# Output stores as planned entries, and a new planned order, in a fused attention and token-mixing kernel

## The chip, the cores and the metric

The kernel runs on one core of a Trainium2 chip. The time is the device time of one execution in microseconds; the median of several runs is shown, and the profile is that of one execution. PE is TensorE (PEld its weight loads), DVE is VectorE, ACT is ScalarE, POOL is GpSimd, and SP is the queue that issues nearly all DMAs here.

## The reference

Two parts, one behind the other. Attention with a sigmoid in place of the softmax, over 8 batches, 12 heads, 448 positions and 64 dimensions; then a token-mixing MLP on its output `x` (8 x 448 x 768):

```python
scores = scale * np.matmul(q, k.transpose(0, 1, 3, 2)) - np.log(S)
attn = 1.0 / (1.0 + np.exp(-scores))
x = np.matmul(attn, v)                      # heads side by side: (B, S, 768)
...
W_tok = scale * np.einsum('bsd,btd->bst', x @ w_q, x @ w_k)
mixed = np.einsum('bst,btd->bsd', W_tok, x)
out = np.maximum(mixed, 0.0) @ w_out
```

Inputs and output are float32. The kernel computes the matrix products in bfloat16 and never forms `W_tok`: it multiplies `x @ w_k` into `x` first (a 64 x 768 product, `tmp`), and then `x @ w_q` into that.

## The kernel before

A batch is a *unit* u (8 of them), four heads are a *quad* j (3 per unit), so there are 24 quads n = 0 to 23. For each quad, q, k and v are loaded as float32 (448 KB each), cast to bfloat16, and q and k are transposed so that the head dimension lies on the partitions. Transposing is done in one of several ways that a letter picks: on PE with a copy out of PSUM (L291, L286, L276), or on DVE in 32 x 32 blocks (L259), for which POOL swaps blocks first (L157 to L163), or on DVE by halves (L252, L228).

Each quad has 7 steps of scores (`scores`, L303: four matmuls on 64 x 64 quarters of the array, then one sigmoid of 128 x 896 on ACT, L308) and 7 steps of values (`values`, L321, summed in PSUM, then a copy to `xt`, L330). So there are 168 sigmoids. Behind a quad, `xt` is transposed back to `xn` (`tr_x`, L344 and L361). Behind a unit come the products of the MLP: `mlp_wqk` (L387, L400), `mlp_wkn` (L416), `mlp_tmp` (L431, copy L435), `mlp_mix` (L471, L483; relu on DVE at L459 or on ACT at L457), and the output blocks (`out_chunk` L600, `out_pair` L516, `out_halves` L556), which are copied out of PSUM into a tile `o` (L525, L633) and stored. There are three such tiles, and in the tail the load buffers `ld` serve as output tiles too.

PSUM is handed out as four pairs of banks in a fixed rotation (`free2`). A step that takes a pair waits until the copy or the sigmoid that read it last has finished.

The order of all work is written out by hand as a string, `PLAN`, one letter for each step: S is a step of scores, P and p one of values (copy on DVE or ACT), q, k and other small letters transposes, X and x `tr_x`, W and L `mlp_wqk`, N, U and M the further products, O and I output blocks (small letter: copy on ACT), C a move of output weights, F a matmul on zeros. Each engine runs its instructions in the order in which the letters emit them and waits only for what it needs. A second string, `ORDER`, gives the order of loads and casts, and a dot in it hands that cast to DVE; the others go to POOL. Loads use a ring of six buffers: the load of entry i is emitted on SP when entry i - 6 has been cast, and so stands in SP's queue between the stores of output blocks. Before, an output block's store is emitted on SP at once behind its copy (L534, L571, L614), so a load that is emitted later waits in SP's queue until that copy has been made.

Of the kernel before, what the change touches and what calls it, by code (L numbers as in the profile page):

```python
# [9 lines left out]
F32 = mybir.dt.float32  # L10
# [7 lines left out]
def kernel(  # L18
# [12 lines left out]
    nc = tc.nc  # L31
    B, H, S, HD = q.shape
    D = H * HD
    DH = moe_w_q.shape[1]
    assert DH == HD == 64 and S == 448 and D == 768
    P = 128
# [83 lines left out]
    def xt(u, j):  # L120
# [4 lines left out]


    PLAN = (
        "SSSFFFFKSqSFFSSkFFSPSPPSpPPPSFSqSkSFPppSPpSpPSabSXSpPSpPSprS"
        "XPPSSFSSWWWSsWzWXWSpPPSpNSppPSqSkSUSXSMSppPSPMppSPSSqkpSSppP"
        "pSpSPWWcSWXSMSdWXSWWSpPSPppNSPPqSkSSUxSMSPPSPppSPPSOOSMSooSq"  # L130
        "kSOoMCSPPCPcSppPPSSdoOSSoXSSOLLScLLLSLpppSPppPSSdoOSOSNxSOcS"
        "UdrSCPSPpSPPPCPpPSPpPSpSsOPSXoSMzSooLSxLSLLLLSPpPSPpPcSPSoXS"
        "SdOOoSpMPSPpCpPSPSoNMSYCOxScPPdppSSooppSPSoOSxScUSLLLSLLdLSp"
        "ppSpPpcPSdoSOMSoSOSMSPpPSPrppSPOmosSoSzooxOSoSOoSoNSOxSOSUSp"
        "PSMcppdPpcpLLLSppLSppLLSPPpOOSdNOSOxOSomoScOOSodSSoOpPmpPpSP"
        "PSOOSoSOtOSoSOMomppPPpmPPOSoxSoSOSLLcLdLLSoSLOSoSOocSoSxoSdO"
        "SppPPSPpSPOSOoNSOoSoSoxSOpPSptpSpPPPppMmPpPpyMWWWWWWxyiNiiti"
        "iiImiImMIiiOoooOoOoOoOOooOO"
    )
    PLAN = "".join(PLAN)  # L140
    KIND = ["a"] + [t for t in PLAN if t in "qacer"]
# [354 lines left out]
    ot = {}  # L496

    opened = []

    def slot(half, b):  # L500

        return b // 2 + (0 if b % 2 == half else NC)

    def out_pair(act):

        if opened:
            w, blocks, part, fb, ps = opened.pop()
        else:
            w, blocks = chunks.pop(0)
            part = 0  # L510
            fb, ps, _ = bank2()
        mx = mxs[w].rearrange("p (u b x) -> p u b x", u=2, b=12)
        for b in range(3 * part, 3 * part + 3):
            for y, (u, i) in enumerate(blocks):
                for x in range(2):
                    nc.tensor.matmul(  # L516
                        ps[HALF[x], y, 0:NB], mx[HALF[y], u, b, 64 * (i - 3 * y) : 64 * (i - 3 * y) + 64],
                        wout16[HALF[y], slot(y, b), x * NB : (x + 1) * NB],
                        start=(b == 0), stop=(b == 11),
                    )  # L520
        if part < 3:
            opened.append((w, blocks, part + 1, fb, ps))
            return
        o = p_o.tile([P, 2, NB], F32, tag="o", name="o")
        COPY["s" if act else "v"](out=o, in_=ps[:, :, 0:NB])  # L525
        release(fb)
        (u0, i0), (u1, i1) = blocks
        for x in range(2):
            cols = slice(x * NB, (x + 1) * NB)
            if u0 == u1:  # L530
                dst = out[2 * w + u0].rearrange("(p i) d -> p i d", i=NI)[:, i0 : i1 + 1 : i1 - i0, cols]
            else:
                dst = out[2 * w : 2 * w + 2].rearrange("b (p i) d -> i p b d", i=NI)[i0, :, :, cols]
            nc.sync.dma_start(out=dst, in_=o[HALF[x]])  # L534

    def out_halves(act):

        if opened:
            w, m, part, fb, ps = opened.pop()
        else:  # L540
            w, m, nb = chunks.pop(0)
            assert nb < 0
            part = 0
            ot[0] = (
                ld_next()[:, 0:D].rearrange("p (b x) -> p b x", b=2) if len(cast) == len(ORDER) + 2
                else p_o.tile([P, 2, NB], F32, tag="o", name="o")
            )
        o = ot[0]
        b, h = divmod(part, 2)
        if not h:  # L550
            fb, ps, _ = bank2()
        for c in range(3 * h, 3 * h + 3):
            t0 = 2 * S * c + m * P + b * NP
            for y in range(2):
                for x in range(2):
                    nc.tensor.matmul(  # L556
                        ps[HALF[x], y, 0:NB], mxs[w][HALF[y], t0 : t0 + NP], wout16[HALF[y], c, x * NB : (x + 1) * NB],
                        start=(c == 0), stop=(c == NC - 1),
                    )
        if h:  # L560
            COPY["s" if act else "v"](out=o[:, b], in_=ps[:, 0, 0:NB])
            nc.vector.tensor_tensor(out=o[:, b], in0=ps[:, 1, 0:NB], in1=o[:, b], op=ALU.add)
            release(fb)
        if part < 3:
            opened.append((w, m, part + 1, fb, ps))
            return
        (b0, i0), (b1, i1) = divmod(2 * m, NI), divmod(2 * m + 1, NI)
        for x in range(2):
            cols = slice(x * NB, (x + 1) * NB)
            if b0 == b1:  # L570
                nc.sync.dma_start(  # L571
                    out=out[2 * w + b0].rearrange("(p i) d -> p i d", i=NI)[:, i0 : i1 + 1, cols], in_=o[HALF[x]],
                )
                continue
            for y, (b, i) in enumerate(((b0, i0), (b1, i1))):
                nc.sync.dma_start(
                    out=out[2 * w + b].rearrange("(p i) d -> p i d", i=NI)[:, i, cols], in_=o[HALF[x], y],
                )

    def out_chunk(act, tail):  # L580

# [10 lines left out]
        last = isinstance(fb, int)  # L592
        if nb == 0 and not part:
            late = w == NU // 2 - 1 and len(cast) == len(ORDER) + 2
            ot[0] = ld_next()[:, 0:D] if late else p_o.tile([P, D], F32, tag="o", name="o")
        o = ot[0]

        def block(ps, w0, w1, c0, c1):
# [35 lines left out]
        release(fb)  # L634
        split = tail and w == NU // 2 - 1 and m == NI - 1
        if nb or split:
            store(slice(nb * NB, (nb + 1) * NB) if split else slice(0, D))

    w32 = {}

# [41 lines left out]
    for n in range(7):  # L682
# [1 line left out]


    ORDER = (
# [5 lines left out]
    )  # L692
    BY = {"s": [], "v": []}
    for x in ORDER.split():
# [5 lines left out]
    ORDER = [(x[0], int(x[1:])) for x in ORDER.replace(".", "").lower().split()]  # L700
    LAG = 9
    issued = {}
    done = dict.fromkeys("SPqkKxWNUMOCgz", 0)
    used, loaded, cast = set(), set(), set()

    ring = [("q", 0), ("k", 0)]
# [105 lines left out]
    for t in PLAN:  # L812
# [14 lines left out]
        if t == "S":  # L827
            scores(*divmod(c, NI))
            cast_by_others()
        elif kind == "P":  # L830
            n, i = divmod(c, NI)
            values(n, i, tail, "s" if t == "p" else "v")
            if i == NI - 1:
                used.add(("v", n))
                pump()
        elif kind in "qk":
            if t in "rs":
                quads_r.append(c) if t == "r" else None
                if t == "s":
                    quadrants(c, 0)  # L840
            tr(c, kind, t)
            if t in "df":
                used.add(("q", c))
            if t not in "cers":
                used.add((kind, c))
                pump()
        elif t == "g":
            move()
        elif t == "z":
            n = quads_r.pop(0)  # L850
            quadrants(n, 1)
            used.update({("q", n), ("k", n)})
            pump()
        elif t == "K":
            tr_part("k", k016, K3, "v")
            tr_part("k", k016, K4, "v")
        elif kind == "x":
            tr_x(c, tail, t in "XY", "s" if t in "yY" else "v")
        elif kind == "W":
            mlp_wqk(*divmod(c, NC), tail, t in "wl", t in "Ll")  # L860
        elif kind == "C":
            for y in range(2):
                nc.sync.dma_start(out=wout16[HALF[y], NC + c, :], in_=wout16[HALF[1 - y], c, :])
        elif kind == "N":
            mlp_wkn(c)
        elif kind == "U":
            (mlp_tmp_tiled if t in "Tt" else mlp_tmp)(c, t in "ut")
        elif kind == "M":
            u, x = divmod(c, NC // 2)
            mlp_mix(u, x, t == "m", tail)  # L870
            if x == NC // 2 - 1:
                if u // 2 in TW:
                    chunks.extend((u // 2, ((u % 2, i), (u % 2, 6 - i))) for i in range(3))
                    if u % 2:
                        chunks.append((u // 2, ((0, 3), (1, 3))))
                else:
                    chunks.extend((u // 2, m, -1) for m in (range(3, NI) if u % 2 else range(3)))
        elif kind == "O":
            if (opened or chunks)[0][0] in TW:
                out_pair(t == "o")  # L880
            elif t in "Ii":
                out_halves(t == "i")
            else:
                out_chunk(t == "o", tail)
    assert not chunks and not opened
# [1 line left out]
_INS = ['q', 'k', 'v', 'moe_w_q', 'moe_w_k', 'moe_w_out']  # L887
_OUTS = [((8, 448, 768), 'float32')]
# [25 lines left out]
```

## Time and profile before

| | |
|---|---|
| median of 3 runs | 187.45 us (186.94 to 189.1) |
| the profiled execution | 187.01 us |
| its span, first to last instruction | 185.3 us |
| instructions | 8549 |
| HBM read, written | 35.78 MB, 11.01 MB |
| clock granted to TensorE | 1.00 |

A row of a group reads: line, engine, operation, out<-in, shapes and count, then busy us and mean ns of one, then the idle time before them and what ended most of it. A row of the timeline reads: start, length, engine, line, operation, tiles, shapes, count, and in brackets the idle time of the engine before it and what released it. A row of the chain reads: start, length, what. A busy PE is not PE at its peak, since matmuls are pipelined.

### The profile page before, as it was taken

How to read it: one execution, taken by the hardware profiler on the slowest of the kernel's cores; microseconds unless marked ns; L12 is line 12 of the kernel's file. 1: busy time of each engine (PE TensorE's matmuls, PEld its weight loads, DVE VectorE, ACT ScalarE, POOL GpSimd, SP SyncE). 2: the span in 40 equal slices, each digit the busy share in tenths (PEclk: the TensorE clock that was granted, in tenths of full speed). 3: DMA queues.
4: the chain of work that ended last, by engine and by line, in shares of the span. 5: the costliest groups of instructions: out<-in, count | busy, mean ns of one | idle time of the engine just before them, and what ended most of it. 6: DMA issues, size and time to landing. Idle time of an engine off the chain costs nothing.

```text
span 185.3 us, 8549 instructions
## 1 busy us (share of the span) xinstructions
PE 174.2 (94%) x3660; PEld 116.8 (63%) x3662; DVE 137.0 (74%) x213; ACT 165.8 (89%) x215; POOL 116.2 (63%) x160
## 2 busy tenths in 40 slices
PE   7887999979989999999999999999999999999990
PEld 7443645544555564656554768768888888879660
DVE  3444787999778899998998999687655885586610
ACT  4798999989989999999999999998999999976540
POOL 1445898699659999799999797969894710000000
PEclk9999999999999999999999999999999999999999
DMA  5999999988998989999999987698388344420696
GB/s 173 360 386 383 285 352 340 388 288 287 375 345 309 283 252 316 367 403 269 300 338 326 264 291 254 203 359 288 115 201 288 80 126 104 117 60 18 165 241 175
DMA packets 26085, 48.51 MB, mean 262 GB/s; under 512 B 3968, under 2 KB 19968, under 8 KB 26048
## 3 DMA queue, kind: packets, MB, share of 16 engines
q1 hardware_dynamic: 25888, 47.79, 79.7%
q8 instruction: 28, 0.46, 1.0%
q10 hardware_dynamic: 160, 0.20, 0.5%
q14 instruction: 9, 0.07, 0.1%
HBM read 35.78 MB, written 11.01 MB: 253 GB/s over the span
## 4 chain that ended last, share of the span: by engine, by line
PE 74%; ACT 12%; DVE 7%; issue 2%; DMA 2%; POOL 0%; ACTq 0%; SPq 0%; DVEq 0%
PE banks L303 15%; PE banks L516 14%; PE banks L321 13%; PE banks L600 12%; ACT at L308 12%; PE banks L387 3%; PE banks L556 3%; PE banks L431 2%; PE banks L344 2%; DMA ld<-in_k_dram 2%; PE banks L361 2%; DVE xt L330 2%; PE banks L400 2%; PE banks L483 1%; PE banks L471 1%
## 5 line engine op out<-in xcount | busy, mean ns | idle before, releaser
L308 ACT ACTIVATE at<-banks 128x896 bf16<-128x896 f32 x168 | 141.1, 929 | 4.5 <-PE banks L303 3.6
L303 PE MATMUL banks<-qk 64*64 64x448 bf16 x672 | 62.6, 357 | 2.8 <-DVE mx L459 0.9
L321 PE MATMUL banks<-at,v 64*64 64x448 bf16 x672 | 45.2, 351 | 0.5 <-ACT at L308 0.2
L303 PEld LDWEIGHTS <-qk 64*64 64x64 bf16 x672 | 25.9, 105 | 20.1 <-issue 11.5
L516 PE MATMUL banks<-wout,mx 64*64 64x384 bf16 x672 | 36.8, 323 | 0.0
L188 POOL CAST qk<-ld 128x896 bf16<-128x896 f32 x25 | 30.5, 1233 | 5.7 <-issue 3.3
L321 PEld LDWEIGHTS <-v 64*64 64x64 bf16 x672 | 23.3, 106 | 9.4 <-issue 2.7
L330 DVE CAST xt<-banks 128x896 bf16<-128x896 f32 x20 | 21.8, 1088 | 7.4 <-PE banks L321 5.6
L516 PEld LDWEIGHTS <-mx 64*64 64x64 bf16 x672 | 24.1, 107 | 3.9
L600 PE MATMUL banks<-wout,mx 128*128 128x384 bf16 (+1 forms) x138 | 24.7, 320 | 0.0
L198 POOL CAST v<-ld 128x896 bf16<-128x896 f32 x22 | 20.6, 949 | 3.6 <-DMA ld<-in_v_dram 2.4
L459 DVE TENSOR_SCALAR mx<-banks 128x1024 bf16<-128x1024 f32 (+2 forms) x19 | 18.6, 987 | 2.3 <-PE banks L471 1.6
L600 PEld LDWEIGHTS <-mx 128*128 128x128 bf16 x138 | 12.0, 97 | 10.7 <-issue 4.5
L157 POOL COPY swap<-qk 32x448 uint32<-32x448 uint32 x26 | 14.7, 564 | 4.9 <-DVE qk L188 3.4
L163 POOL COPY qk<-swap 32x448 uint32<-32x448 uint32 x26 | 15.3, 590 | 1.5
L259 DVE STREAM_TRANSPOSE qk<-qk 128x448 f32<-128x448 f32 x26 | 16.0, 628 | 0.0
L525 DVE COPY o<-banks 128x768 f32<-128x768 f32 x12 | 11.5, 955 | 5.9 <-PE banks L516 3.6
L160 POOL COPY qk<-qk 32x448 uint32<-32x448 uint32 x26 | 14.8, 567 | 1.5
L374 DVE COPY xn<-banks 128x1024 bf16<-128x1024 bf16 (+1 forms) x14 | 8.7, 630 | 2.2 <-PE banks L361 2.0
L457 ACT ACTIVATE mx<-banks 128x448 bf16<-128x448 f32 (+1 forms) x11 | 8.1, 768 | 0.5 <-PE banks L483 0.5
L387 PE MATMUL banks<-xt,wqk 64*64 64x448 bf16 x120 | 8.0, 351 | 0.0
L198 POOL CAST q<-ld 128x896 bf16<-128x896 f32 x6 | 5.6, 932 | 3.8 <-DMA ld<-in_q_dram 2.3
(94 smaller groups left out, 212.6 us busy)
## 6 DMA issues: line engine op xcount, KB each, us to landing
ld<-in_q_dram SPq DMA_DIRECT2D x24, 448.0 KB, 6.0
ld<-in_v_dram SPq DMA_DIRECT2D x24, 448.0 KB, 6.1
ld<-in_k_dram SPq DMA_DIRECT2D x23, 448.0 KB, 6.3
out_dram<-o SPq DMA_DIRECT2D x42, 192.0 KB, 4.7
ld<-in_moe_w_out_dram SPq DMA_DIRECT2D x6, 384.0 KB, 5.7
out_dram<-ld SPq DMA_DIRECT2D x11, 192.0 KB, 2.8
wout<-wout SPq DMA_DIRECT2D x12, 96.0 KB, 5.7
out_dram<-ld SPq DMA_DIRECT2D x4, 96.0 KB, 2.6
```

Of the source, the lines that this page charges most:

```text
L160: eng.tensor_copy(out=w[hi, 0], in_=w[lo, 1])
L163: eng.tensor_copy(out=w[lo, 1], in_=z[lo])
L188: COPY[e](out=f[:, :, "qk".index(nm)].rearrange("p e i d y -> p e y i d"), in_=ld.pop((nm, n)).rearrange("p (y i e d) -> p e y i d", y=2, ...
L198: COPY[e](out=t16.rearrange("p i b d -> p b i d"), in_=ld.pop((nm, n)).rearrange("p b (i d) -> p b i d", i=NI),)
L259: nc.vector.transpose(out=qk[n][:, t].rearrange("p t i n -> p (t i n)").bitcast(F32), in_=w)
L303: nc.tensor.matmul(sc[HALF[h], g, 0:S], qk[n][HALF[g], h, 1, i, :], qk[n][HALF[g], h, 0].rearrange("p i n -> p (i n)"), start=True, stop=True,
L308: nc.scalar.activation(at, sc[:, :, 0:S], ACTF.Sigmoid, bias=attn_bias, scale=attn_scale)
L321: nc.tensor.matmul(ps[HALF[g], h, 0:S], ld["v16", n][HALF[h], i, g, :], ats[n, i][HALF[h], g, :], start=(i == 0), stop=(i == NI - 1),)
L330: COPY[eng](out=xt(u, j)[:, :, 0:S], in_=ps[:, :, 0:S])
L459: nc.vector.tensor_scalar(dst, ps, moe_scale, 0.0, ALU.mult, ALU.max)
L516: nc.tensor.matmul(ps[HALF[x], y, 0:NB], mx[HALF[y], u, b, 64 * (i - 3 * y) : 64 * (i - 3 * y) + 64], wout16[HALF[y], slot(y, b), x * NB : ...
L600: nc.tensor.matmul(ps, mxs[w][:, 2 * S * c + m * P : 2 * S * c + (m + 1) * P], wout16[:, c, w0:w1], start=(c == 0), stop=(c == NC - 1),)
```

## The change

Three things. Stores of output blocks become entries of their own in `PLAN`, with the letter D: `out_pair`, `out_halves` and `out_chunk` no longer issue the store but put it on a list, and D issues the oldest. When a new `o` tile is wanted whose buffer a waiting store still reads, that store is issued first; in the tail stores are issued at once. `PLAN` is another string (647 letters, with 21 D, in place of 627). `ORDER` is another string, with 19 casts on DVE in place of 14. The counts of the other steps stay; some copies change between DVE and ACT, and one quad is transposed by POOL swaps and L259 in place of halves.

```diff
+    stores, o_tiles = [], [0]
+
+    def flush(n=None):
+
+        for _, f in stores[:n]:
+            f()
+        del stores[:n]
+
+    def o_tile(shape):
+
+        while stores and stores[0][0] <= o_tiles[0] - 3:
+            flush(1)
+        o_tiles[0] += 1
+        return p_o.tile(shape, F32, tag="o", name="o")
...
-        o = p_o.tile([P, 2, NB], F32, tag="o", name="o")
+        o = o_tile([P, 2, NB])
         COPY["s" if act else "v"](out=o, in_=ps[:, :, 0:NB])
         release(fb)
...
+        stores.append((o_tiles[0] - 1, store))
+        if tail:
+            flush()
...
+        elif kind == "D":
+            flush(1)
```

The beginning of the two plans and of the two orders of loads, and the order's last lines:

```diff
-        "SSSFFFFKSqSFFSSkFFSPSPPSpPPPSFSqSkSFPppSPpSpPSabSXSpPSpPSprS"
-        "XPPSSFSSWWWSsWzWXWSpPPSpNSppPSqSkSUSXSMSppPSPMppSPSSqkpSSppP"
+        "SSSFFFFFKSSqFFSSkFFSSSSPPpSPppPFqSkSPPPSSppPPSabSXSrSpPppSPS"
+        "DpXSPSSFSSWWsWWzXWWSpPSPPPpNSPqSkSSDUSXSMDSpPPMSPppSPSqkSWSW"
...
-        "q1 .k1 v0 v1 .q2 k2 q3 k3 v2 k4 q4 w0 q5 v3 q6 k5 v4 q7 v5 w5 "
-        ".k6 q8 k7 .w4 .k8 k9 v6 v7 v8 w3 q9 q10 w6 .k10 w1 w2 k11 .v9 "
+        "q1 .k1 v0 q2 k2 v1 k3 q3 v2 q4 k4 w0 v3 v4 q5 k5 v5 q6 q7 k6 w3 "
+        "k7 .k8 .w1 v6 k9 q8 v7 q9 w5 q10 w4 v8 .k10 w2 .w6 .v9 q11 k11 "
...
-        "q21 q22 q23 v20 .v21 v22 v23 k22 .k23 "
+        ".q17 k16 .k17 q18 v16 k18 .k19 q19 k20 v17 v18 .k21 q20 .q21 "
+        ".q22 k22 v19 .v20 q23 v21 .v22 .k23 .v23 "
```

More of the change, by code (lines that the diff above doesn't have):

```diff
@@ L127 @@
     PLAN = (
-        "SSSFFFFKSqSFFSSkFFSPSPPSpPPPSFSqSkSFPppSPpSpPSabSXSpPSpPSprS"
-        "XPPSSFSSWWWSsWzWXWSpPPSpNSppPSqSkSUSXSMSppPSPMppSPSSqkpSSppP"
[L130 to L138, printed above, removed]
+        "SSSFFFFFKSSqFFSSkFFSSSSPPpSPppPFqSkSPPPSSppPPSabSXSrSpPppSPS"
+        "DpXSPSSFSSWWsWWzXWWSpPSPPPpNSPqSkSSDUSXSMDSpPPMSPppSPSqkSWSW"
+        "WcpSpPSppPSPXSWSSdWMXSWSppppSPpNPSqSkSUSxSMPSppPSpSPPSOOSMSO"
+        "oqSkSOOPSMCpSPPppSPDSOcOdDSSOXSLLLSOcSLLpSLppSPpPPSSodOSxSoN"
+        "CSCOCSPPcdSUSPpSDCPrpPpPSpppsSpSCOPSXoSMSOoLzSxLSLDLLSLppSPp"
+        "cPSpPSOodSSOXoMSpPPcSPpPSPSoNMSYOSxSDdoDOPSpPSppSPPOOSxDSUSL"
+        "cLLSSLdLLpPpPSppPcSOSoMSOSOSMPPSPppPDdmOPSoSOSOSOcONSdoxSOOS"
+        "OSxoSOSUSpcpSMPPPPplllSPlDpSdpPlDxlpppDOSoSoSOOSDOcSModSooSO"
+        "OcNSOmTpPpSpPPpSOMoSodSOSOODSPDPSOPPSpPPmOOoDSomcLOSLdLLSLLo"
+        "SoDSoSOSOcodSDOxSOPpSppSPNpPODoSxSoOSoSOxSOSOtPpSPSppPMPPppP"
+        "mPPPMwwwwwwxxIyNiiTiIiImiimmiIIooOOoooooOOoooOO"
     )
@@ L498, with out_pair @@
     opened = []
+    stores, o_tiles = [], [0]
[8 more added lines that the diff above has]
+        return p_o.tile(shape, F32, tag="o", name="o")
     def slot(half, b):
         return b // 2 + (0 if b % 2 == half else NC)
-    def out_pair(act):
+    def out_pair(act, tail):
         if opened:
@@ L527, in out_pair, with store, out_halves @@
         (u0, i0), (u1, i1) = blocks
[L528 to L536, printed above, removed]
+        def store():
+            for x in range(2):
+                cols = slice(x * NB, (x + 1) * NB)
+                if u0 == u1:
+                    dst = out[2 * w + u0].rearrange("(p i) d -> p i d", i=NI)[:, i0 : i1 + 1 : i1 - i0, cols]
+                else:
+                    dst = out[2 * w : 2 * w + 2].rearrange("b (p i) d -> i p b d", i=NI)[i0, :, :, cols]
+                nc.sync.dma_start(out=dst, in_=o[HALF[x]])
+        stores.append((o_tiles[0] - 1, store))
+        if tail:
+            flush()
+    def out_halves(act, tail):
         if opened:
@@ L545, in out_halves @@
                 ld_next()[:, 0:D].rearrange("p (b x) -> p b x", b=2) if len(cast) == len(ORDER) + 2
-                else p_o.tile([P, 2, NB], F32, tag="o", name="o")
+                else o_tile([P, 2, NB])
             )
@@ L567, in out_halves, with store @@
         (b0, i0), (b1, i1) = divmod(2 * m, NI), divmod(2 * m + 1, NI)
[L568 to L578, printed above, removed]
+        def store():
+            for x in range(2):
+                cols = slice(x * NB, (x + 1) * NB)
+                if b0 == b1:
+                    nc.sync.dma_start(
+                        out=out[2 * w + b0].rearrange("(p i) d -> p i d", i=NI)[:, i0 : i1 + 1, cols], in_=o[HALF[x]],
+                    )
+                    continue
+                for y, (b, i) in enumerate(((b0, i0), (b1, i1))):
+                    nc.sync.dma_start(
+                        out=out[2 * w + b].rearrange("(p i) d -> p i d", i=NI)[:, i, cols], in_=o[HALF[x], y],
+                    )
+        stores.append((o_tiles[0] - 1, store))
+        if tail or len(cast) == len(ORDER) + 2:
+            flush()
     def out_chunk(act, tail):
@@ L594, in out_chunk @@
             late = w == NU // 2 - 1 and len(cast) == len(ORDER) + 2
-            ot[0] = ld_next()[:, 0:D] if late else p_o.tile([P, D], F32, tag="o", name="o")
+            ot[0] = ld_next()[:, 0:D] if late else o_tile([P, D])
         o = ot[0]
@@ L636, in out_chunk @@
         if nb or split:
-            store(slice(nb * NB, (nb + 1) * NB) if split else slice(0, D))
+            stores.append((o_tiles[0] - 1, lambda: store(slice(nb * NB, (nb + 1) * NB) if split else slice(0, D))))
+            if tail or w == NU // 2 - 1 and (m == NI // 2 or len(cast) == len(ORDER) + 2):
+                flush()
     w32 = {}
@@ L702 @@
     issued = {}
-    done = dict.fromkeys("SPqkKxWNUMOCgz", 0)
+    done = dict.fromkeys("SPqkKxWNUMOCDgz", 0)
     used, loaded, cast = set(), set(), set()
@@ L879 @@
             if (opened or chunks)[0][0] in TW:
-                out_pair(t == "o")
+                out_pair(t == "o", tail)
             elif t in "Ii":
-                out_halves(t == "i")
+                out_halves(t == "i", tail)
             else:
                 out_chunk(t == "o", tail)
-    assert not chunks and not opened
+    assert not chunks and not opened and not stores
 _INS = ['q', 'k', 'v', 'moe_w_q', 'moe_w_k', 'moe_w_out']
```

3 rows, old and new, of the table ORDER are left out of this document.

## The prediction

> **What bounds the kernel now.** I read the page from the top: busy shares, the chain of waits, a table of four stretches, and the timeline where the chain leaves one engine for another.
>
> ```profile
> span 185.3 us, 8549 instructions
> PE 174.2 (94%) x3660; PEld 116.8 (63%) x3662; DVE 137.0 (74%) x213; ACT 165.8 (89%) x215; POOL 116.2 (63%) x160
> PE 74%; ACT 12%; DVE 7%; issue 2%; DMA 2%; POOL 0%; ACTq 0%; SPq 0%; DVEq 0%
> L308 ACT ACTIVATE at<-banks 128x896 bf16<-128x896 f32 x168 | 141.1, 929 | 4.5 <-PE banks L303 3.6
> 6.20:50.00 43.80, 38.95 (x811) 21.63 (x805) 32.23 (x44) 42.58 (x52) 31.80 (x39) 1.00 0.99 344
> 50.00:110.00 60.00, 59.22 (x1084) 34.29 (x1087) 54.48 (x75) 59.02 (x75) 52.18 (x70) 1.00 0.95 315
> 110.00:161.90 51.90, 51.90 (x1372) 42.50 (x1365) 36.52 (x53) 49.98 (x62) 30.70 (x45) 1.00 0.65 195
> 161.90:185.30 23.40, 19.01 (x364) 14.03 (x358) 11.08 (x23) 11.75 (x25) 0.00 (x0) 1.00 0.52 132
> ...
> 107.61 0.92 ACT at L308
> 112.92 0.97 PE banks L516 x22
> ```
>
> The stretches give length, then busy time of PE, PEld, DVE, ACT and POOL, the clock, and DMA. Until 110 us ScalarE is the metronome: it is busy 42.58 of 43.80 and 59.02 of 60.00 us, mostly with the 168 sigmoids. The last long ScalarE piece of the chain is at 107.61 us; the long pieces behind it are matmuls. From 110 us PE has no gap (51.90 of 51.90 us) while DVE falls to 36.52. So there are two regimes. In front, time is won only where ScalarE stands or steps slowly. Behind, only by fewer matmuls or by coming to that stretch sooner. VectorE is close to a bound in front, with 54.48 of 60.00 us.
>
> The two built programs have the same 7326 PE instructions, the same loads and stores and 168 sigmoids, in another order. No PE work is saved, so the sum goes by ScalarE's lost time in front, and by stands that the new order makes.
>
> **Where ScalarE loses time in front.**
>
> ```profile
> 6.22 11.73 ACT L308 ACTIVATE at<-banks 128x896 bf16<-128x896 f32 x14 [0.48 <-PE banks L303]
> 18.50 20.42 ACT L308 ACTIVATE at<-banks 128x896 bf16<-128x896 f32 x25 [0.55 <-PE banks L303]
> 39.16 0.92 ACT L308 ACTIVATE at<-banks 128x896 bf16<-128x896 f32 x1 [0.23 <-PE banks L303]
> 40.35 11.58 ACT L308 ACTIVATE at<-banks 128x896 bf16<-128x896 f32 x14 [0.28 <-PE banks L303]
> 52.60 5.95 ACT L308 ACTIVATE at<-banks 128x896 bf16<-128x896 f32 x7 [0.67 <-PE banks L303]
> ```
>
> A merged row's last sigmoid starts 0.92 us before the row's end. The 25 from 18.50 us step by (20.42 - 0.92) / 24 = 0.81 us: the undisturbed pace. Three places fall behind it. The first 14 step by (11.73 - 0.92) / 13 = 0.83, and the 15th starts 18.50 - 17.03 = 1.47 us behind the 14th: 0.9 us lost in all. Around 39 us the steps are 39.16 - 38.00 = 1.16 and 1.19: 0.7 us. At 52.60 the step is 52.60 - 51.01 = 1.59: 0.8 us.
>
> **Part 1: loads and casts in a new order.** The first place:
>
> ```profile
> 11.20 0.93 POOL L198 CAST v<-ld 128x896 bf16<-128x896 f32 x1 [0.27 <-DMA ld<-in_v_dram]
> 15.39 0.94 POOL L198 CAST k<-ld 128x896 bf16<-128x896 f32 x1 [3.26 <-DMA ld<-in_k_dram]
> 12.44 0.63 DVE L198 CAST q<-ld 128x896 bf16<-128x896 f32 x1 [1.05 <-DMA ld<-in_q_dram]
> 16.38 0.41 PE L212 MATMUL banks<-ident,k 64*64 64x64 bf16 x28 [0.93 <-POOL k L198]
> 16.92 1.09 DVE L291 COPY qk<-banks 128x1792 bf16<-128x1792 bf16 x1 [1.92 <-ACT at L308]
> ```
>
> POOL waits 3.26 us for k2 to land, PE waits for that cast, and L291 (its copy is what the 15th scores read) follows 0.13 us behind the transposes. These loads are of one size, so landings go by the slot in SP's queue. Before, slots four to six hold v1 (cast at 11.20), q2 (12.44) and k2 (15.39); after, q2, k2 and v1. So k2 can be cast from about 12.4 us, 3 us sooner, and v1 takes the late slot and is done at 16.3. The values of quad 0 move as well, behind the 11th and 12th scores, so k2's transposes are now set by PE's order: an estimated 16.1 us for their end. L291 adds 1.09 and the scores 0.4, so the 15th sigmoid starts near 17.7 instead of 18.50. The change adds a wait: three value steps of quad 1 stand ahead of the 15th scores in PE's queue and wait for v1 until 16.3; at four matmuls in 0.2 us each they are done at 16.9, under the 17.3 of L291. That cover is 0.4 us; without it the gain shrinks by as much as v1 is later. Gain taken: 0.8 us.
>
> The second place:
>
> ```profile
> 35.94 1.21 POOL L188 CAST qk<-ld 128x896 bf16<-128x896 f32 x1
> 36.06 1.57 DVE L198 CAST k<-ld 128x896 bf16<-128x896 f32 x1
> 38.68 0.38 PE L303 MATMUL banks<-qk 64*64 64x448 bf16 x4 [0.94 <-DVE mx L459]
> ```
>
> The cast of k6 on VectorE stands between two L459 copies; the second releases the banks that the scores wait for. After the change k6 is cast by POOL, and nothing stands between the two. What is late next is VectorE's own queue there (xt, then L291 of the next quad).
>
> The third place: at 52.60 the scores wait behind the matmuls of L431, which themselves stand 0.42 us; the chain there reads:
>
> ```profile
> 50.85 0.42 issue
> 51.28 0.66 PE banks L431 x5
> ```
>
> In the new plan a step of scores stands between L431 and the transposes of xt, which before followed it at once. The second and third place hold 0.7 + 0.8 = 1.5 us. I take half, 0.75: the new order also packs two mode changes of PE, a mix and a transpose between the 47th and 48th scores, whose crowding no row of this trace prices; I bound it by 0 and by the 0.8 us of the stands just read.
>
> **Part 2: stores as entries of their own.** A store now stands up to 10 scores behind its copy, and loads may pass it on SP; no more than three output tiles are open, since the oldest store is issued first when a fourth is wanted.
>
> ```profile
> 137.63 0.96 DVE L525 COPY o<-banks 128x768 f32<-128x768 f32 x1 [1.67 <-DMA out_dram<-o]
> out_dram<-o SPq DMA_DIRECT2D x42, 192.0 KB, 4.7
> ```
>
> Before, one copy waited for a store, 1.67 us, inside the stretch in which PE has no gap: it cost nothing. After, the ninth tile (copied after the 122nd scores) is stored after the 132nd and needed again at the 136th. There the scores step by about 1.06 us (51.90 us for 49), and 4 steps are 4.2 us against 4.7 for a landing. So a copy on VectorE may wait 0 to 1.7 us, with L459, xt and the next output copy behind it, whose banks PE wants. In the early half the loads that pass the stores come sooner, by at most a store's place in the queue; POOL's waits there are off the chain (POOL 0%). I take 0 for both: SP goes through its list as its waits end, often earlier than the place in the plan, and the one case seen was free.
>
> Instruction reads:
>
> ```profile
> PEld L303 <- issue: 11.5, 35, 1.2
> q8 instruction: 28, 0.46, 1.0%
> ```
>
> If the 28 reads caused all 11.5 us of PEld's unexplained standing, a plan that avoids them could win up to that in front; but ScalarE stands only 4.5 us in all, three places of which are counted above. Taken: 0. The Trainium skill (Runtime: NRT & Kernel Launch, Instruction fetch mechanics) says that sequential instruction fetch is mostly hidden behind the issue rate, which gives the same 0; no row here ties a stand to a read.
>
> **Part 3: 19 casts on VectorE in place of 14.**
>
> ```profile
> L188 DVE CAST qk<-ld 128x896 bf16<-128x896 f32 x7 | 6.7, 970 | 0.0
> L228 DVE STREAM_TRANSPOSE qk<-qk 32x448 f32<-32x448 f32 x12 | 7.6, 636 | 0.3
> L633 ACT COPY o<-banks 128x384 f32<-128x384 f32 x6 | 3.0, 492 | 0.0
> ```
>
> Through the 120th scores both orders have 12 casts on VectorE. The five more, 5 x 0.97 = 4.9 us, all lie behind, where VectorE has 51.90 - 36.52 = 15.4 us free; one quad fewer by halves takes 4 x 0.64 = 2.5 us off. Hidden, unless they come in one block: two follow the 134th scores and three the 148th. ScalarE copies one output half less in front, 0.4 us off (its 0.49 less the overlap). PE's remaining work at the 120th, 144th and 168th scores differs by a few value steps, so the rear keeps its length.
>
> **The sum.** 0.8 + 0.75 + 0.4 = 1.95 us off. The profiled execution took 187.01 us, 1.7 us of it around the span; the median of the runs is 187.45, 0.44 above. 187.01 - 1.95 + 0.44 = 185.5 us.
>
> **Rivals.** *New stands for old.* ScalarE's lost time is moved, not removed: with VectorE at 54.48 of 60.00 us, 2 us less length means 94% busy, and its in-order queue passes every slip to the banks. Against it: the places above are read from this trace and the new order does treat each. It gives 187.0.
>
> *Blocks of casts stop PE (slower).* At the 134th and 148th scores two and three casts stand in a row, with output and xt copies behind them whose banks PE needs. A cast took 0.97 us on average and 1.57 beside a POOL cast; at the mean of these, 1.27, the blocks are 2.5 and 3.8 us. One step of 1.06 is covered by the other banks, so PE stands 1.5 + 2.7 = 4.2 us, and 185.5 + 4.2 = 189.7. At 0.97 it is 2.7 us and 188.2; from 1.18 us a cast on, it is over 1% slower. Against it: four bank pairs may cover more than one step. The Trainium skill (SBUF — State Buffer, SBUF: two separate sides) has VectorE and GpSimd hold a shared port pair exclusively for a whole instruction, which speaks against more VectorE casts while POOL works. By that rule, the trace agrees: 1.57 us beside POOL.
>
> *More than counted.* All 1.5 us of the second and third place go, and the loads gain something further on: 183.9 us or less.
>
> **How the numbers follow.** Forecast 0.47, about 184.4 to 186.8; new stands 0.26; blocks of casts 0.19; more than counted 0.08. One per cent, about what a measurement of this kernel can tell, is 185.6 and 189.3 us. Faster: 0.27 of the forecast and 0.08 make 0.35. Slower: 0.14 of the blocks. Same: 0.20 + 0.26 + 0.05 = 0.51. The range leaves out half of the best case and the upper part of the blocks: 183.8 to 189.4.
>
> **What would show it.** Right: the 15th sigmoid starts at 17.5 to 17.9 us, POOL's 3.26 us wait is on v, no step over 1.1 us near the 39th and 55th sigmoid, and the 120th starts 1.5 to 2.5 us before 110.8. Wrong: the 120th no earlier; or PE with gaps of a microsecond between 125 and 160 us, on L525 or L330, behind L188 or a store.

## The result, and the profile after

| | before | changed |
|---|---|---|
| median | 186.96 us (20 runs) | 188.38 us (20 runs) |
| profiled execution | 187.01 us, span 185.3 | 189.17 us, span 187.4 |

The changed kernel takes 1.0092 times as long, with a 95% interval of 1.0062 to 1.0121. 185.5 was forecast; it came out 1.4 us slower than before instead of some 2 us faster. All medians here are taken over every run, while ratios leave out disturbed runs, so the two can differ a little.

Lines of the changed kernel are numbered higher (L516 is L530, L525 is L539, L600 is L626, L633 is L659); L303, L308 and L431 keep theirs. The page of the changed kernel, with the rows that answer to those of before:

```profile
span 187.4 us, 8548 instructions
...
PE 175.3 (94%) x3660; PEld 116.4 (62%) x3662; DVE 140.1 (75%) x218; ACT 164.0 (88%) x211; POOL 115.0 (61%) x161
...
q8 instruction: 28, 0.46, 1.0%
...
PE 68%; DMA 16%; ACT 4%; POOL 3%; issue 3%; DVE 3%; SPq 1%; ACTq 0%; POOLq 0%
...
L308 ACT ACTIVATE at<-banks 128x896 bf16<-128x896 f32 x168 | 141.3, 929 | 7.4 <-PE banks L303 6.9
...
L303 PEld LDWEIGHTS <-qk 64*64 64x64 bf16 x672 | 25.6, 105 | 21.3 <-issue 13.2
```

ScalarE's idle time before a sigmoid grew from 4.5 to 7.4 us, nearly all behind the scores on PE. The loads that the chain names (DMA 16%, 2% before) all lie ahead of 40 us, where it is followed back through POOL's casts rather than the sigmoids; they say nothing on the time behind 40 us. To see where, here are four stretches of the changed kernel (length, then busy time of PE, PEld, DVE, ACT and POOL, the clock, DMA share, GB/s):

```profile
45.00:53.00 8.00, 6.92 (x190) 4.10 (x194) 6.31 (x10) 7.23 (x10) 4.41 (x6) 1.00 0.95 349
105.00:110.00 5.00, 4.10 (x92) 2.62 (x87) 3.81 (x5) 3.98 (x6) 4.46 (x8) 1.00 0.88 316
126.00:136.00 10.00, 8.36 (x202) 6.28 (x198) 7.04 (x11) 8.03 (x11) 7.39 (x11) 1.00 0.87 298
...
110.00:162.00 52.00, 50.36 (x1331) 40.82 (x1327) 39.68 (x55) 47.90 (x58) 28.53 (x41) 1.00 0.67 197
```

The first three of the kernel before:

```profile
45.00:53.00 8.00, 7.33 (x183) 4.04 (x182) 5.91 (x9) 7.33 (x10) 4.97 (x7) 1.00 1.00 365
105.00:110.00 5.00, 4.84 (x111) 3.46 (x104) 4.82 (x6) 5.00 (x7) 3.91 (x5) 1.00 0.87 287
126.00:136.00 10.00, 10.00 (x280) 8.56 (x273) 6.93 (x10) 9.45 (x12) 9.09 (x13) 1.00 0.57 180
```

PE now stands inside the stretch that had no gap: 8.36 of 10.00 us, with 202 matmuls where 280 ran, at the same full clock. The DMA engines are 0.87 to 0.95 busy in all three; in the third they were at 0.57 before. In the first two they were as busy before (1.00 and 0.87), so their busy share alone does not make PE stand. The chain of waits of the changed kernel shows what the standing looks like (start, length, what):

```profile
48.83 0.77 PE banks L431 x7
49.60 0.54 issue
50.14 0.32 PE banks L431
...
106.39 0.18 PE banks L303 x3
106.57 0.73 issue
107.30 0.36 PE banks L303
...
127.00 0.18 PE banks L303 x3
127.19 0.80 issue
127.98 0.35 PE banks L303
...
133.21 0.12 PE banks L416 x7
133.33 0.84 issue
134.18 0.19 PE banks L416
```

Each stand lies in the middle of a group: three matmuls of four or seven of eight are done, then PE waits for nothing that the profile shows, and then the last one runs. No copy and no bank can do that, since a group waits for its banks at its first matmul. Counted in pairs of weight load and matmul, the four come in front of pairs 864, 1888, 2400 and 2528; all are 96 past a multiple of 128. So each lies at a multiple of 256 PE instructions from the others (a pair is two), and the span holds 28 instruction reads of 16 KB for 7,322 PE instructions, one for each 262. The trace of DMA ties the reads to these places. The changed kernel's PE passes such a boundary at 100.54 us; the two windows below are 100.5 to 104.8 us and 104.8 to 105.9 us (queue: packets, MB, share of the 16 engines):

```profile
q1 hardware_dynamic: 371, 1.14, 83.8%
...
q1 hardware_dynamic: 133, 0.30, 86.7%
q8 instruction: 1, 0.02, 5.4%
```

For 4.3 us only loads and stores move. Then comes one instruction packet (104.87 to 105.82 us); PE reaches the next boundary at 106.2 and goes on at 107.30, 1.5 us behind the end of the packet. So the block was used up before the next was there. Measured between two weight loads, the four stands are 1.16, 1.08, 1.20 and 0.96 us, 4.4 us in all. (Of the first, 0.31 us is the gap that the same place has where PE doesn't stand, in e2 below.) The kernel before shows one, 0.77 us at pair 864: it is the "0.42 issue" at 50.85 that the prediction quotes.

From 110 to 162 us the changed kernel's PE lacks 52.00 - 50.36 = 1.64 us, and the two stands of that stretch in the chain are 0.80 + 0.84 = 1.64 us: no store, cast or copy made PE stand there. The three stands behind 100 us, which the kernel before doesn't have, are 2.37 us in the chain, and the span is 2.1 us longer.

### The profile page after: what moved, and what is told of

It is laid out like the page before. It is cut to its first block, busy times and chain, and to the rows that moved or that the text cites. A ratio compares the mean times of both kernels' runs of the same rounds, so it can differ in the third digit from the quotient of the medians.

```text
span 187.4 us, 8548 instructions
## 1 busy us (share of the span) xinstructions
PE 175.3 (94%) x3660; PEld 116.4 (62%) x3662; DVE 140.1 (75%) x218; ACT 164.0 (88%) x211; POOL 115.0 (61%) x161
## 4 chain that ended last, share of the span: by engine, by line
PE 68%; DMA 16%; ACT 4%; POOL 3%; issue 3%; DVE 3%; SPq 1%; ACTq 0%; POOLq 0%
PE banks L530 14%; PE banks L303 14%; PE banks L321 12%; PE banks L626 12%; DMA ld<-in_k_dram 7%; DMA ld<-in_q_dram 5%; DMA ld<-in_v_dram 4%; ACT at L308 3%; PE banks L387 3%; PE banks L576 3%; PE banks L431 2%; PE banks L361 2%; PE banks L471 1%; PE banks L344 1%; PE banks L447 1%
## 5 line engine op out<-in xcount | busy, mean ns | idle before, releaser
L308 ACT ACTIVATE at<-banks 128x896 bf16<-128x896 f32 x168 | 141.3, 929 | 7.4 <-PE banks L303 6.9
L303 PE MATMUL banks<-qk 64*64 64x448 bf16 x672 | 63.5, 358 | 3.9 <-issue 1.5
L303 PEld LDWEIGHTS <-qk 64*64 64x64 bf16 x672 | 25.6, 105 | 21.3 <-issue 13.2
L530 PE MATMUL banks<-wout,mx 64*64 64x384 bf16 x672 | 36.4, 323 | 0.0
L188 POOL CAST qk<-ld 128x896 bf16<-128x896 f32 x21 | 25.5, 1222 | 7.3 <-issue 4.2
L530 PEld LDWEIGHTS <-mx 64*64 64x64 bf16 x672 | 23.7, 107 | 6.5 <-issue 2.5
L330 DVE CAST xt<-banks 128x896 bf16<-128x896 f32 x19 | 20.6, 1086 | 7.0 <-PE banks L321 6.5
L626 PE MATMUL banks<-wout,mx 128*128 128x384 bf16 (+1 forms) x138 | 24.9, 321 | 0.2 <-ACT at L308 0.2
L459 DVE TENSOR_SCALAR mx<-banks 128x1024 bf16<-128x1024 f32 (+2 forms) x20 | 19.9, 1000 | 2.3 <-PE banks L471 0.9
L198 POOL CAST v<-ld 128x896 bf16<-128x896 f32 x20 | 18.8, 951 | 2.6 <-DMA ld<-in_v_dram 2.3
L157 POOL COPY swap<-qk 32x448 uint32<-32x448 uint32 x28 | 15.9, 570 | 5.1 <-DVE qk L188 3.6
L626 PEld LDWEIGHTS <-mx 128*128 128x128 bf16 x138 | 11.9, 98 | 10.4 <-issue 4.6
L163 POOL COPY qk<-swap 32x448 uint32<-32x448 uint32 x28 | 16.7, 598 | 1.6
L539 DVE COPY o<-banks 128x768 f32<-128x768 f32 x13 | 12.4, 956 | 7.0 <-PE banks L530 5.0
L259 DVE STREAM_TRANSPOSE qk<-qk 128x448 f32<-128x448 f32 x28 | 17.4, 630 | 0.0
L188 DVE CAST qk<-ld 128x896 bf16<-128x896 f32 x11 | 9.0, 842 | 0.1
L198 POOL CAST q<-ld 128x896 bf16<-128x896 f32 x7 | 6.8, 978 | 2.3 <-DMA ld<-in_q_dram 2.3
```

Source lines behind the costliest of these rows:

```text
L157: eng.tensor_copy(out=z[lo], in_=w[hi, 0])
L163: eng.tensor_copy(out=w[lo, 1], in_=z[lo])
L188: COPY[e](out=f[:, :, "qk".index(nm)].rearrange("p e i d y -> p e y i d"), in_=ld.pop((nm, n)).rearrange("p (y i e d) -> p e y i d", y=2, ...
L198: COPY[e](out=t16.rearrange("p i b d -> p b i d"), in_=ld.pop((nm, n)).rearrange("p b (i d) -> p b i d", i=NI),)
L259: nc.vector.transpose(out=qk[n][:, t].rearrange("p t i n -> p (t i n)").bitcast(F32), in_=w)
L303: nc.tensor.matmul(sc[HALF[h], g, 0:S], qk[n][HALF[g], h, 1, i, :], qk[n][HALF[g], h, 0].rearrange("p i n -> p (i n)"), start=True, stop=True,
```

## The experiments

Theory A is that the change puts loads and stores under way where PE fetches its next block, so that the reads come late and PE stands. Its rivals are parts of the change themselves: the stores, the casts on VectorE, or the new order (the last is the rival that was hardest to tell apart). Stands are listed where they are over 0.4 us at such a boundary, measured between weight loads. The column "15 to 168" is the time from the start of the 15th to the start of the last sigmoid in the profiled execution, and behind it the same less the stands.

| run | edit to | median us (runs) | ratio to before | profiled span | stands, sum | 15 to 168 | less stands |
|---|---|---|---|---|---|---|---|
| before | | 186.96 (20) | | 185.3 | 1, 0.77 | 142.44 | 141.67 |
| changed | | 188.38 (20) | 1.0062 to 1.0121 | 187.4 | 4, 4.40 | 145.46 | 141.06 |
| e1 | changed | 188.37 (10) | 1.0008 to 1.0108 | 186.7 | 3, 3.42 | 144.49 | 141.07 |
| e2 | changed | 187.55 (10) | 1.0018 to 1.0104 | 184.4 | none | 141.53 | 141.53 |
| e3 | before | 189.79 (4) | 1.002 to 1.0266 | 189.4 | 2, 4.19 | 147.20 | 143.01 |
| e4 | before | 187.53 (10) | 0.9978 to 1.0061 | 184.5 | 2, 1.15 | 142.63 | 141.48 |
| e5 | changed | 188.06 (6) | 1.0046 to 1.0181 | 186.0 | 1, 1.26 | 142.61 | 141.35 |
| e6 | before | 186.23 (12) | 0.9976 to 1.0046 | 184.3 | none | 141.32 | 141.32 |
| e7 | changed | 187.59 (6) | 1.0037 to 1.0181 | 185.6 | none | 142.57 | 142.57 |
| e8 | e4 | 189.12 (6) | 1.0052 to 1.0201 | 186.5 | 2, 3.34 | 144.62 | 141.28 |
| e9 | changed | 185.69 (8) | 0.9936 to 0.9981 | 184.5 | 1, 0.43 | 141.69 | 141.26 |
| e10 | before | 185.48 (11) | 0.9909 to 0.9954 | 183.7 | none | 141.59 | 141.59 |
| e12 | changed, again | 188.03 (1) | | 186.2 | 2, 2.50 | 143.93 | 141.43 |

The last column is 141.1 to 141.7 us in eleven of the thirteen profiles, whichever order they run: between these two sigmoids the stands carry the differences, and neither order is faster without them. The two exceptions are e3, which has 3.4 us at half the clock, and e7, which loses 0.9 us at the 60th to 62nd sigmoid, where no boundary stand lies. A second count over the same thirteen profiles ties the stands to the reads: each has one read for each boundary, PE never passed the next boundary sooner than 1.23 us after the end of that read's packet, and all 18 stands of the table ended 1.24 to 1.75 us after it.

The kernel before had medians of 187.11 (beside e1 to e4), 187.24 (e5 to e8) and 186.78 us (e9 to e12), and the ratios are to these.

**e1: each store at once behind its copy**, in the changed order (shown for `out_pair`; the two other functions are edited alike).

```diff
         stores.append((o_tiles[0] - 1, store))
-        if tail:
-            flush()
+        flush()
```

> The changed kernel with every store issued at once behind its copy, as before the change; plan, casts and all else as changed. Theory A (late instruction reads): PE stands about 1 us each time the next 256 of its instructions arrive late, at pairs 864, 1888, 2400 and 2528 of weight load and matmul (96 modulo 128). The read for pair 2400 started 3.55 us behind the block's start with six stores under way; with the stores spread it starts earlier, the stands at 2400 and 2528 shrink to under 0.5 us each, and the time falls by 1 to 2 us against the changed kernel, to about 186.5. Those at 864 and perhaps 1888 stay. Theory B (blocks of casts on VectorE stop PE): no change, 188.4.

188.37 us, as the changed kernel, with three of the four places still standing; the 1 to 2 us that Theory A expected to win did not come. The stores as entries of their own neither make the loss nor save anything that shows.

**e2: the last three casts of v back on POOL.**

```diff
-        ".q22 k22 v19 .v20 q23 v21 .v22 .k23 .v23 "
+        ".q22 k22 v19 v20 q23 v21 v22 .k23 v23 "
```

> The changed kernel with the casts of v20, v22 and v23 given to POOL, so that VectorE has no block of three casts behind the 148th scores. Theory A: the stands at pairs 1888, 2400 and 2528 lie before that place or do not hang on it; the time stays within 0.7 us of the changed kernel. Theory B: 1 to 2.7 us faster.

187.55 us, with an interval that overlaps that of the changed kernel: not told apart. Its profiled execution was its fastest run (186.16 us) and has no stand at all, not even that at pair 864, though nothing was changed ahead of 110 us. So the stands come and go from one execution to the next. From 126 to 136 us the DMA engines are 0.92 busy there and PE is busy for 10.00 of 10.00 us: a busy DMA does not always make a read late enough.

**e3: more transfers, and nothing else**, in the kernel before: three loads of 448 KB, which nobody reads, behind the 127th scores.

```diff
+            if c == 126:
+                for h in range(3):
+                    nc.sync.dma_start(
+                        out=extra[h], in_=SRC["q"][h, 0:4].rearrange("h (p r) d -> (h p) (r d)", r=2 * NI),
+                    )
```

> The kernel before with three more loads of 448 KB into tiles that nothing reads, put in SP's queue behind the 127th scores. Theory A: an instruction read near 125 us starts about 3 us later than its 2.5 us, PE stands 1 to 3 us at a pair that is 96 modulo 128 (2400 or 2528), with no semaphore that ends the stand, and the time grows by 1 to 3 us. Theory B, or any theory in which only buffers and engines count: PE's pairs are not held there, and the time grows by less than 0.5 us, unless a late v cast is named as what ended the wait.

The median of four runs rose to 189.79 us (188.31, 188.48 and twice 191.1; the interval of the ratio is wide). The chain of waits of its profiled execution (lines are numbered 2 higher here):

```profile
115.50 0.19 PE banks L305
115.69 2.03 issue
117.72 0.53 PE banks L305
...
129.58 0.13 PE banks L363 x8
129.71 1.77 issue
131.48 0.35 PE banks L363 x21
```

Both are in front of pairs at block boundaries (2144 and 2400), and the reads for them began 4.0 and 4.7 us after the start of the blocks that ran out. The order of the engines' work is that of before, so added transfers alone make PE stand. Not all of the longer time is standing: behind the first stand the granted clock was 0.51 for 3.4 us, which no other profile of the table shows between the 15th and the last sigmoid (the third number from the end is the clock).

```profile
117.80:121.20 3.40, 3.40 (x65) 2.35 (x64) 0.89 (x2) 1.83 (x2) 2.75 (x5) 0.51 0.96 324
```

**e4: only the new front**, the first line of `PLAN` (with the loads that go with it) up to quad 3, in the kernel before.

```diff
-        "SSSFFFFKSqSFFSSkFFSPSPPSpPPPSFSqSkSFPppSPpSpPSabSXSpPSpPSprS"
+        "SSSFFFFFKSSqFFSSkFFSSSSPPpSPppPFqSkSPPPSSppPPSabSXSpPSpPSprS"
...
-        "q1 .k1 v0 v1 .q2 k2 q3 k3 v2 k4 q4 w0 q5 v3 q6 k5 v4 q7 v5 w5 "
+        "q1 .k1 v0 q2 k2 v1 k3 q3 v2 q4 k4 w0 q5 v3 q6 k5 v4 q7 v5 w5 "
```

> The kernel before with the changed kernel's order up to the transposes of quad 3 alone (q2 and k2 ahead of v1, first values later, q2 cast by POOL). Step of the prediction: the 15th sigmoid starts near 17.8 us in place of 18.5, and if the front sets the end the time falls by 0.5 to 0.9 us. Theory A adds that the blocks of instructions meet other transfers, so the rest may move by a stand of about 1 us either way.

The 15th sigmoid started at 17.56 us, and no change of the time could be measured: 1.0019, 0.9978 to 1.0061. A gain of 0.8 us, the largest term of the prediction, would be 0.9957 and is out; one of 0.4 us is not.

**e5 and e6: no loads of q, k and v of quads 15 to 23**, in the changed kernel and in the one before. Their casts read what lies in the tiles.

```diff
         u, j = quads[n]
+        if n >= 15:
+            ld[nm, n] = ld_next() if KIND[n] in "cer" and nm != "v" else ld_next2()
+            return
```

> The changed kernel without the loads of q, k and v of quads 15 to 23: their steps run on what the buffers hold, all engine work and all stores stay. Theory A (late instruction reads): with the transfers of the stretch from about 85 to 140 us gone, reads start within 2.5 us of the block's start, no stand over 0.4 us is left at pairs 1888, 2400 and 2528, and the time is about 185.5 us, no slower than its counterpart e6. Theory C (the new order of the rear is itself slower, by its stores, casts or copies): the time falls alike in both, and this one stays 1 to 2 us above e6.

> The kernel before without the same loads. Theory A: it has few stands in that stretch to lose, so it falls by at most 0.7 us, to about 186.3, and ends level with e5 or 0.3 to 0.9 us above it. Theory C: 1 to 2 us below e5.

No stand is left behind 100 us in either. By the ratios neither kernel gained anything that can be measured (1.0011 for before, 0.9976 to 1.0046), and the changed kernel stayed 1.8 us above, as the rival said. That spoke for the order itself, but one stand was left: 1.26 us in front of pair 864, where loads still ran. It is most of the difference of the two profiled spans, 1.7 us; the rest lies behind the last sigmoid. What a boundary looks like without transfers is seen in e5 at 94.44 us, in the window 94.4 to 95.7 us:

```profile
DMA packets 1, 0.02 MB, mean 13 GB/s; under 512 B 0, under 2 KB 0, under 8 KB 0
...
q8 instruction: 1, 0.02, 5.9%
```

The only packet is the instruction read, and it starts at 94.45 us, 0.01 behind the boundary.

**e7 and e8: six warm-up matmuls fewer**, which shifts every block boundary by six pairs against the work, in the changed kernel and in e4.

```diff
-    for _ in range(32):
+    for _ in range(26):
```

> The changed kernel with 26 warm-up matmuls on zeros in place of 32, so that every block of 256 PE instructions starts six pairs later in the work. Theory A: any stand of a microsecond without a named releaser is again at a pair that is 96 modulo 128, so at other matmuls than before (six later in the work); the time moves by up to 1 us, either way. Theory C: stands stay at the same matmuls of the plan, and the time stays within 0.4 us of the changed kernel.

> The kernel before with the new head (e4) and 26 warm-up matmuls. Theory A: the 15th sigmoid near 17.6 us as in e4, the stands of 0.5 to 0.6 us at pairs 2144 and 2528 of e4 change; if they go, the time is 0.5 to 1 us under the kernel before, the only one of these that beats both. Theory C: as e4, within 0.3 us of the kernel before.

Inconclusive. e7 lost the stands, but its 15th sigmoid started 1.1 us later than the changed kernel's, and it came out at 187.59. e8 had new stands of 1.90 and 1.44 us, at pairs 2144 and 2272, again 96 past a multiple of 128, and came out at 189.12, 1.6 us above e4.

**e9 and e10: no loads of quads 10 to 23**, to take the transfers away around 45 us too. The edit is that of e5 with 10 for 15.

> Leaves out the loads of q, k and v of quads 10 to 23 (their tiles hold what lay there before, so the outputs differ). TensorE stood 1.26 us at 49.3 us in the run without the loads of quads 15 to 23, behind an instruction read that began 3.5 us after its block while three loads of MoE weights and three of quads were under way. Theory A (late instruction reads carry the whole of the lost time): with fewer loads there the read begins under 2.5 us after the block, the stand at 49.3 us falls under 0.4 us, TensorE's idle time to about 3.5 us, and the time to 186.0 to 187.0, that of the same edit to the kernel before within 0.7 us. Rival (the new order itself costs, in the places of its copies and transposes): the time stays over 187.5 and over 1 us above the same edit to the kernel before.

> The kernel before without the loads of q, k and v of quads 10 to 23. It had no stand left without those of quads 15 to 23 (186.23). Theory A: 185.8 to 186.6, nothing more to win, so that the two kernels meet. Rival (the order itself costs): the same here, but the changed kernel stays over 1 us above it.

The two kernels meet: 185.69 and 185.48 us. From the single runs the means differ by 0.17 us (-0.17 to 0.50), where the whole change costs 1.42. The stand at pair 864 fell to 0.43 us. One stretch each, of e9 and of e10:

```profile
110.00:162.00 52.00, 51.92 (x1368) 41.73 (x1360) 40.86 (x57) 49.54 (x62) 28.96 (x41) 1.00 0.45 106
```

```profile
110.00:162.00 52.00, 52.00 (x1396) 42.75 (x1386) 36.82 (x53) 50.18 (x63) 29.50 (x42) 1.00 0.43 105
```

In the changed kernel PE was busy for 50.36 us of the same 52. The rival, over 187.5 us, is out. What could be left of it is small: in e9 a weight load of PE waits 0.45 us at 132.8 us for a cast of v on POOL, which e10 doesn't have. The edit also takes away every wait for the landing of these loads, so by themselves the two runs don't part late reads from late loads; the stands without a releaser, and the ends of the packets, do.

**e11: at most five loads under way**, through five tiles.

```diff
-        return lds[(nld[0] - 1) % 6]
+        return lds[(nld[0] - 1) % (5 if nld[0] <= 80 else 6)]
```

> The changed kernel with its loads through five tiles instead of six, so that at most five loads are under way; nothing is left out. Theory A: the reads wait behind a shorter row of loads and start some 0.5 to 0.7 us earlier where the row was full; stands of about 1.1 us shrink to some 0.5, and the time to 187.0 to 187.8, unless the casts now wait for their loads. Rival (loads an entry later make casts late): sigmoids wait for scores in the first 60 us, 189.5 or more. If the order itself costs: 188.4, no change.

This test failed: 238.25 us. The loads stay six entries ahead of the casts, so a load goes into a tile whose cast stands behind it in the program; some casts read later data, contrary to the expectation's "nothing is left out", and POOL waits 10.1 us in all for loads of q. It says nothing on the theory.

**e12: the changed kernel once more**, for a second profile.

> The changed kernel once more, for a second profile. Theory A: the stands move from one execution to the next, since the delay of a read hangs on what is under way just then: one to four of them, each at one of the same block boundaries (near 49, 106, 127 and 133 us, or another), and the span is 184 to 185 us plus about the sum of the stands. Rival (the order itself costs): the same span above the sum of the stands, 186 or more with none.

188.03 us. The two stands over 0.4 us, in its chain of waits:

```profile
49.92 0.92 issue
...
132.18 0.84 issue
```

Measured between weight loads they are 1.55 (pair 864) and 0.95 us (pair 2528); at the other two places no stand is over 0.4 us.

## Why the prediction was wrong

Two steps failed: the time that ScalarE lost in front was taken for a property of the order, so most of the 1.55 us taken off for it was not there to win; and instruction reads were put at nothing, where the changed kernel's profile has 4.4 us of stands. The rival of blocks of casts, at 188.2 to 189.7 us, comes near the measured 188.38, but by luck: its mechanism did not occur.

**Instruction reads, "Taken: 0": this step failed.** The prediction had the row (11.5 us of PEld's waits on "issue") and the argument that ScalarE stands only 4.5 us. That bounds what a plan could win by avoiding late reads; it does not bound what a plan can lose by making more of them late. The two profiles of the changed kernel have four and two stands, 4.4 and 2.5 us, where that of before has one of 0.77. The sentence "no row here ties a stand to a read" was true only of the rows looked at: a stand in the middle of a group, at a multiple of 256 instructions from the next, is such a row. The Trainium skill (Runtime: NRT & Kernel Launch, Instruction fetch mechanics) has sequential fetch mostly hidden. The changed kernel's profile agrees for 24 of its 28 reads, which no stand over 0.4 us follows; four stands of 0.96 to 1.20 us follow the others, so "mostly" does not give 0.

**The first place, 0.8 us: seen, and worth nothing.** The sign was right: the 15th sigmoid started at 17.82 us, and the sigmoids run through, as the changed kernel's timeline shows:

```profile
13.67 36.45 ACT L308 ACTIVATE at<-banks 128x896 bf16<-128x896 f32 x44
50.88 6.70 ACT L308 ACTIVATE at<-banks 128x896 bf16<-128x896 f32 x8 [0.77 <-PE banks L303]
```

(44 sigmoids at 0.83 us each.) But the price was read from one execution. The old front is also in e6 and e10, whose missing loads come much later. Their timelines, e6 first (lines are 3 higher):

```profile
14.12 0.94 POOL L201 CAST k<-ld 128x896 bf16<-128x896 f32 x1 [1.56 <-DMA ld<-in_k_dram]
...
13.29 26.07 ACT L311 ACTIVATE at<-banks 128x896 bf16<-128x896 f32 x32
```

```profile
13.89 0.94 POOL L201 CAST k<-ld 128x896 bf16<-128x896 f32 x1 [1.59 <-DMA ld<-in_k_dram]
...
13.73 24.49 ACT L311 ACTIVATE at<-banks 128x896 bf16<-128x896 f32 x30
```

POOL waits 1.6 us for k2 there, not 3.26, and 32 or 30 sigmoids follow one another without a break, the 15th among them. So k2 landed late in the one execution that was profiled, and the 0.8 us were not the order's to win. The plainest case is e3, which has the plan and the loads of before up to the 127th scores; its 15th sigmoid started at 17.62 us, sooner than the changed kernel's (L310 is L308 there):

```profile
12.84 41.66 ACT L310 ACTIVATE at<-banks 128x896 bf16<-128x896 f32 x51
```

This row runs to 54.50 us, so it holds all three places of the prediction, and none of them is there. Contrary to the forecast, POOL's long wait did not move to v1 in the changed kernel; it is gone (v1 is cast at 13.54 us after a wait of 0.18).

**The second and third place, 0.75 us.** Around 39 us the sigmoids now run through, as forecast; in the order of before they do so too in e3, while e10 has steps of 1.14 and 1.20 us there, so this place comes and goes. The third place was misread: the stand of L431 at 50.85 was a late instruction read, which a step of scores behind L431 does not touch. The changed kernel's sigmoid comes 1.68 us behind the one before it there, where the prediction read 1.59; in e3, e4, e6 and e10, which have no stand at pair 864, the step is 0.88 us in the order of before.

**One output copy less on ScalarE, 0.4 us.** ScalarE does make five of these copies in place of six; the time that it is worth can't be told from the rest.

**Stores, 0 us: right as far as the runs show** (e1). **Casts, hidden: right as well.** In the changed kernel itself the two stands make up all of PE's lost time from 110 to 162 us, and e9 has all 19 casts on VectorE with PE at 51.92 of 52 us. So blocks of casts did not stop PE here; that rival is out, and it was the only one on the slower side.

**The sign "the 120th sigmoid 1.5 to 2.5 us earlier" was badly chosen.** By the count that has the 15th at 18.50 us, the sigmoid at 110.8 us is the 121st; it came at 112.33 us, 1.5 us later. The stand of 1.08 us at 106 us lies ahead of it, and so does a relu of 1.02 us on ScalarE (L457, at 110.59 us), which the order of before has just behind it (at 111.64 us). In e2, which has no stand, the new order takes 6.15 us from the 115th to the 121st sigmoid, against 4.9 before. The index of a sigmoid is no measure of the work done when two orders differ. The other sign of being wrong, PE gaps of a microsecond between 125 and 160 us, did come, on no copy or store but in the middle of groups.

**What is shown and what is argued.** Shown: added transfers make PE stand at block boundaries (e3); without the later loads the two kernels take the same time (e9, e10); and less the stands, the time from the 15th to the last sigmoid is the same in both orders to 0.6 us, but for e3 and e7. That the instruction read is the link is read from place and time in the traces, without an exception in thirteen profiles, but nothing here delayed a read without other transfers. Why the new order makes reads late more often stays open: which of the many moved loads matters was not tried one by one, and at pair 864 the reads of both kernels were about as late (3.5 us).

## What to carry to other kernels

When an engine stands in the middle of a group and no releaser is named, count its instructions between such stands: a fixed step points to its instruction reads, and the transfers under way at that time are the suspects. A new order that moves loads or stores has a price there that no wait in the old trace shows, so bound it on the slower side. A wait for a landing that is read from a single execution is not yet a property of the order: look for the same place in a second profile before taking it off the sum. Here all three places that were to be won are missing from e3, whose order is that of before up to there.

## What the runs showed of the hardware

The read of the next PE block starts about when PE passes a boundary: 0.01 us later with nothing under way (e5 at 94.44 us), but 3.2 to 4.7 us later in front of the stands over 0.9 us, with the DMA engines 0.84 busy in the window shown. The packet then takes about 1 us, and PE goes on 1.2 to 1.8 us after its end. In the changed order the block in front of pair 864 lasts about 5 us: reads that started 3.5 to 4.0 us late left a gap of 1.16 to 1.61 us there, one 2.84 us late (e9) left 0.43, and one 1.9 us late (e2) 0.31, which is no stand.
